# Sums of both halves of the queries and both heads of a pair on four column tiles, an earlier second load, and two moves around the mixer

## Chip, cores, metric

One NeuronCore of a Trainium2 chip. The metric is device microseconds (us) of one execution. Each figure is a median of several executions; most executions of one kernel agree within 0.3%. "Half clock" below means stretches in which the trace records a granted clock of TensorE of 0.5.

## The reference, cut to what matters

```python
# hash attention: B=4, H=8 heads, S=768, D=64, 6 hash bits
mask   = bucket(q @ proj)[..., :, None] == bucket(k @ proj)[..., None, :]
scores = where(mask, q @ k.T / 8, -1e9)
attn   = exp(scores - max);  attn = attn / (sum(attn) + 1e-9)
x      = (attn @ v) as (B, S, 512)
# mixer
u   = x + (relu(x.T @ w_tok1) @ w_tok2).T      # token mixing
out = u + relu(u @ w_ch1) @ w_ch2              # channel mixing
```

## The kernel before, in the parts that matter

Attention goes over 16 pairs of heads (two heads side by side on the 128 partitions), and in each pair over two halves of 384 queries. For a half, TensorE makes scores in six chunks of keys, ScalarE takes the exponentials `e`, GpSimd and VectorE add the six chunks (`esa`, `esd`), TensorE sums over keys with a matrix of ones (`sums`), ScalarE and VectorE turn this into a factor by logarithm, exponential and one Newton step, TensorE weighs the values (`acc`), ScalarE moves `acc` to `num`, and GpSimd multiplies `num` by the factor into `XT`. Sums and weighing of a half are issued during the next half.

```python
            def sums(self):
                ps = psum.tile([P, 512], F32, name="sums", tag="sm", bufs=1)[:, :HALF]
                for i in range(2):                                   # the two heads
                    nc.tensor.matmul(ps[D*i : D*i+D], ones, self.d[:, i], start=True, stop=True)
                # near = exp(-ln(ps)) on ScalarE
            def newton(self):
                # rec = (ps * near - 2) * near: two VectorE operations of 128x384
...
        for n in range(len(pairs)):
            for half in range(2):
                now = Half(n, half); now.scores()
                now.add(0)                      # GpSimd: e0+e1; VectorE: e2+e3+e4
                if before: before.sums()
                if half == 0 and n + 1 < len(pairs):
                    hashes(n + 1)               # ends in 8 small transfers of bits on the SP queue
                    load_qk(n + 2)
                ...
                if before: before.newton()
                now.add(1)                      # VectorE: +e5, then +esa
                if n:
                    weights.some(third)         # a third of one weight block's conversion
                    third = (third + 1) % 3
                if before: before.weigh()       # TensorE acc, ScalarE num, GpSimd division
```

The weights arrive as 64-bit floats and are converted in blocks of 768 KB, one third of the work in each half:

```python
        def begin(self):   # third 0: ScalarE reads raw (the block that has landed), VectorE two operations
        def join(self):    # third 1: VectorE, then GpSimd two operations of 128x768
        def end(self):     # third 2: ScalarE a square, VectorE the last operation (L196), which frees raw
        def some(self, k):
            (self.begin, self.join, self.end)[k]()
            if k == 2:
                self.fetch()                    # request of the next block into the only raw buffer
```

So the request of a block waits for VectorE's L196, and one half later ScalarE, an in-order queue, must have the block before it may move `acc` or take exponentials.

## Time and profile before

886.32 us, median of three runs; the profiled one has a span of 883.2 us. By stage:

| stretch, us from the start | length | TensorE busy | granted clock |
|---|---|---|---|
| 0 to 27.93 (to the first sums) | 27.93 | 18.1 | 0.88 |
| to 347.32 (attention) | 319.39 | 317.6 | 1.00 |
| to 442.47 (token mixing) | 95.15 | 91.7 | 1.00 |
| to 883.20 (channel mixing) | 440.73 | 433.6 | 1.00 |

The start is the one stretch with large gaps. The prediction shows the lines behind this.

### The profile page before, as it was taken

The numbers are of one execution on the slowest core, as the hardware profiler recorded it, in microseconds if no ns is written. First come the engines' busy times: TensorE is split into PE (matmuls) and PEld (weight loads), VectorE is DVE, ScalarE is ACT, GpSimd is POOL, SyncE is SP. The second block draws the span as 40 slices with busy tenths as digits, with TensorE's granted clock in tenths as the row PEclk, the third lists the DMA queues.
The fourth block names the chain that finished last, engine by engine and source line by source line (L and its number), as shares of the span: only waits on it lengthen the run. The fifth ranks groups of instructions, "written<-read, shape, count | busy, mean of one in ns | idle before, by whom it ended". The sixth has DMA issues, their size and how long they took to land.

```text
span 883.2 us, 9198 instructions
## 1 busy us (share of the span) xinstructions
PE 861.0 (97%) x3505; PEld 394.2 (45%) x3505; DVE 494.6 (56%) x576; ACT 321.4 (36%) x477; POOL 243.8 (28%) x156
## 2 busy tenths in 40 slices
PE   5999999999999999999999999999999999999997
PEld 2444444444444445455534444444444444444443
DVE  2666776776677554589975464435448342336411
ACT  2676776667777665424311210001210101211000
POOL 3253544354444222547611111101111200111110
PEclk9999999999999999999999999999999999999999
DMA  5223323322322203223301211131120120000001
GB/s 177 79 75 110 112 87 151 126 99 85 111 110 75 74 3 108 71 72 108 107 1 36 72 36 60 52 127 38 70 71 1 59 84 24 0 1 0 24 24 51
DMA packets 20500, 61.14 MB, mean 69 GB/s; under 512 B 2785, under 2 KB 4193, under 8 KB 20449
## 3 DMA queue, kind: packets, MB, share of 16 engines
q1 hardware_dynamic: 20392, 60.46, 19.8%
q8 instruction: 29, 0.48, 0.2%
q14 instruction: 23, 0.18, 0.1%
q10 hardware_dynamic: 56, 0.02, 0.0%
HBM read 53.49 MB, written 6.29 MB: 68 GB/s over the span
## 4 chain that ended last, share of the span: by engine, by line
PE 90%; DVE 4%; DMA 2%; ACT 1%; issue 1%; SPq 1%; POOL 0%; DVEq 0%; ACTq 0%
PE b L587 48%; PE sc L299 16%; PE acc L363 13%; PE t L522 4%; PE sums L343 3%; PE t L535 2%; PE hp L266 2%; DMA qk<-in_qk 1%; PE trp L226 1%; SPq L280 1%; DMA raw<-in_moe_w_tok 1%; DVE XT L541 1%; DVE WC L196 1%; DVE tmp L170 1%; ACT e L306 1%
## 5 line engine op out<-in xcount | busy, mean ns | idle before, releaser
L299 PE MATMUL sc<-qk 64*128 64x384 f32 x768 | 161.9, 501 | 2.5 <-ACT e L306 2.5
L306 ACT ACTIVATE e<-sc 128x768 f32<-128x768 f32 x192 | 150.4, 813 | 28.7 <-PE sc L299 28.7
L594 ACT COPY p<-b 128x512 f32<-128x512 f32 x72 | 42.2, 586 | 295.5 <-PE b L587 295.5
L363 PE MATMUL acc<-e,vn 128*64 128x384 f32 x768 | 130.0, 488 | 0.0
L587 PE MATMUL b<-r,WC 128*128 128x512 f32 x288 | 125.6, 592 | 0.0
L587 PE MATMUL b<-T,SW 128*128 128x512 f32 x216 | 97.0, 593 | 1.7 <-DVE T L677 0.9
L299 PEld LDWEIGHTS sc<-qk 64*128 64x128 f32 x768 | 67.8, 190 | 61.1 <-issue 45.9
L331 DVE TENSOR_TENSOR esd<-e 128x768 f32<-128x768 f32 x32 | 41.2, 1289 | 93.5 <-ACT e L306 93.5
L613 POOL TENSOR_TENSOR p<-p,p 128x512 f32<-128x512 f32 x18 | 25.5, 1415 | 238.9 <-ACT p L594 238.9
L363 PEld LDWEIGHTS acc<-e,vn 128*64 128x64 f32 x768 | 53.9, 137 | 72.4 <-issue 72.2
L587 PEld LDWEIGHTS b<-r,WC 128*128 128x128 f32 x288 | 54.7, 190 | 68.9 <-issue 66.5
L329 POOL TENSOR_TENSOR esa<-e 128x768 f32<-128x768 f32 x32 | 66.4, 2076 | 33.7 <-ACT e L306 33.7
L371 POOL TENSOR_TENSOR XT<-num,rec 128x384 f32<-128x384 f32 x32 | 39.1, 1221 | 125.8 <-ACT num L368 87.5
L587 PE MATMUL b<-T,WC 128*128 128x512 f32 x144 | 67.7, 593 | 0.1
L587 PEld LDWEIGHTS b<-T,SW 128*128 128x128 f32 x216 | 40.9, 190 | 54.0 <-issue 50.7
L185 POOL TENSOR_TENSOR tmp<-tmp,raw 128x768 f32<-128x768 f32 x20 | 41.0, 2052 | 86.0 <-DVE tmp L182 48.8
L587 PE MATMUL b<-XT,WC 128*128 128x512 f32 x144 | 64.7, 592 | 0.0
L299 PE MATMUL sc<-bits 64*128 64x384 bf16 x384 | 63.5, 324 | 0.0
L587 PE MATMUL b<-r,SW 128*128 128x512 f32 x144 | 62.8, 592 | 0.0
L617 DVE TENSOR_TENSOR r<-p,u 128x512 f32<-128x512 f32 x18 | 12.5, 692 | 87.2 <-ACT u L594 86.7
L368 ACT ACTIVATE num<-acc,vsum 128x384 f32<-128x384 f32 x32 | 18.6, 580 | 71.2 <-PE acc L363 71.2
L535 PE MATMUL t<-W,r 128*128 128x384 f32 x128 | 42.3, 488 | 1.6 <-DVE XT L541 1.6
(81 smaller groups left out, 955.5 us busy)
## 6 DMA issues: line engine op xcount, KB each, us to landing
raw<-in_moe_w_ch SPq DMA_DIRECT2D x16, 768.0 KB
seen<-in_qk SPq DMA_DIRECT2D x16, 768.0 KB
qk<-in_qk SPq DMA_DIRECT2D x15, 768.0 KB
vn<-in_v SPq DMA_DIRECT2D x16, 384.0 KB
vt<-in_vT SPq DMA_DIRECT2D x16, 384.0 KB
out<-p SPq DMA_DIRECT2D x18, 256.0 KB
raw<-in_moe_w_tok SPq DMA_DIRECT2D x4, 768.0 KB
bits<-g SPq DMA_DIRECT2D x124, 5.2 KB
```

What stands on the lines that cost most here:

```text
L185: nc.gpsimd.tensor_tensor(unit, unit, lo, op=ALU.mult)
L299: nc.tensor.matmul(sc[:, i, :HALF], t[rows, 1, P * c : P * c + P], t[rows, 0, qs], start=start, stop=not start,)
L306: nc.scalar.activation(e, sc[:, :, :HALF], ACT.Exp, scale=SCALE)
L329: nc.gpsimd.tensor_tensor(self.a, es[0], es[1], op=ALU.add)
L331: nc.vector.tensor_tensor(self.d, es[2], es[3], op=ALU.add)
L343: nc.tensor.matmul(ps[D * i : D * i + D], ones, self.d[:, i], start=True, stop=True,)
L363: nc.tensor.matmul(acc[D * i : D * i + D], vn[:, i, c], e[:, i], start=(c == 0), stop=(c == NR - 1),)
L371: nc.gpsimd.tensor_tensor(XT[:, hp, at : at + HALF], num, self.rec, op=ALU.mult)
L522: nc.tensor.matmul(ps, W1[:, r, P * j : P * j + P], x[:, r], start=(r == 0), stop=(r == NR - 1),)
L535: nc.tensor.matmul(ps[:, :HALF], r1[:, j, P * cb : P * cb + P], W2[:, j, HALF * half : HALF * half + HALF], start=(j == 0), stop=(j == NJ ...
L587: nc.tensor.matmul(self.ps[i], left(k), right(k), start=first and k == ks[0], stop=k == ks[-1], skip_group_check=True,)
L594: nc.scalar.copy(c, self.ps[i])
```

## The change

Its intent: fill four column tiles of TensorE with sums instead of two, so that one pass does both halves of a pair; take the second pair's load out of TensorE's way; keep TensorE's clock open with idle matmuls at the start; make two of the four block differences of channel mixing during token mixing; and shorten the tail. Cut to its core:

```diff
-            def sums(self):            # once per half: 2 matmuls of 64 columns
+        class Quotients:               # once per pair, in the first half of the next pair
+            def sums(self):
+                for i in range(2):
+                    for h in range(2):
+                        at = 32 * (2 * i + h)
+                        nc.tensor.matmul(ps[at:at+32], ones[:, :32], self.halves[h].d[:, i], ...)
+            def newton(self):
+                nc.vector.tensor_tensor(t, ps, near, op=ALU.mult)
+                for h in range(2):
+                    nc.vector.scalar_tensor_tensor(rec[:, h], t, 2.0, near, ...)
+                for i in range(2):
+                    for h in range(2):
+                        at, other = D*i + 32*h, D*i + 32*(1-h)
+                        nc.vector.tensor_copy(rec[other:other+32, h], rec[at:at+32, h])
+            def divide(self):          # one GpSimd operation of 128x768 instead of two of 128x384
+                nc.gpsimd.tensor_tensor(XT[...], nums.pop(self.n), self.rec, op=ALU.mult)
...
+        load_qk(1)                     # ahead of the first bits' transfers, was behind load_v(0)
+        idle = psum.tile(...)
+        for _ in range(14):
+            nc.tensor.matmul(idle[:D, :D], ones, ones, start=True, stop=True)
...                                     # token mixing, after its third batch:
+            if b == 2:
+                inputs(0, T, 0)        # two of four differences; T is now four tiles, was one
...                                     # last output block:
+                for cols in parts:     # two halves of 256 columns
+                    x.product(3, ..., cols)
```

More of the change, by code (lines that the diff above doesn't have):

```diff
@@ L78 @@
     assert S == 6 * P and DM == 512 and NB <= 8 and DTOK % P == 0 and DCH % P == 0
-    assert B * NP % 2 == 0 and B * S % (2 * TT) == 0
+    assert 2 * TT <= 2 * S and B > 2 and B * NP % 2 == 0 and B * S % (2 * TT) == 0
     SCALE = 0.125
@@ L329, in add @@
                     nc.gpsimd.tensor_tensor(self.a, es[0], es[1], op=ALU.add)
-                    self.d = pool.tile([P, 2, HALF], F32, name="esd", tag="esd", bufs=2)
+                    self.d = pool.tile([P, 2, HALF], F32, name="esd", tag="esd", bufs=3)
                     nc.vector.tensor_tensor(self.d, es[2], es[3], op=ALU.add)
@@ L337, in add @@
                     )
-            def sums(self):
-                ps = psum.tile([P, 512], F32, name="sums", tag="sm", bufs=1)[:, :HALF]
-                for i in range(2):
-                    nc.tensor.matmul(
-                        ps[D * i : D * i + D], ones, self.d[:, i], start=True, stop=True,
-                    )
-                near = pool.tile([P, HALF], F32, name="near", tag="near", bufs=2)
-                nc.scalar.activation(near, ps, ACT.Ln)
-                nc.scalar.activation(near, near, ACT.Exp, scale=-1.0)
-                self.ps, self.near = ps, near
-            def newton(self):
-                ps, near = self.ps, self.near
-                rec = self.rec = pool.tile([P, HALF], F32, name="rec", tag="rec", bufs=2)
-                nc.vector.tensor_tensor(rec, ps, near, op=ALU.mult)
-                nc.vector.scalar_tensor_tensor(rec, rec, 2.0, near, op0=ALU.subtract, op1=ALU.mult)
             def weigh(self):
@@ L366, in weigh, with __init__ @@
                         )
-                num = pool.tile([P, HALF], F32, name="num", tag="num", bufs=2)
-                nc.scalar.activation(num, acc, ACT.Identity, scale=-1.0, bias=vsum)
+                if self.half == 0:
+                    nums[self.n] = pool.tile([P, 2, HALF], F32, name="num", tag="num", bufs=2)
+                nc.scalar.activation(
+                    nums[self.n][:, self.half], acc, ACT.Identity, scale=-1.0, bias=vsum,
+                )
+        nums = {}
+        class Quotients:
+            def __init__(self, halves):
+                self.n, self.halves = halves[0].n, halves
+            def sums(self):
+                ps = psum.tile([P, 512], F32, name="sums", tag="sm", bufs=1)[:, :HALF]
+                for i in range(2):
+                    for h in range(2):
+                        at = 32 * (2 * i + h)
+                        nc.tensor.matmul(
+                            ps[at : at + 32], ones[:, :32], self.halves[h].d[:, i], start=True, stop=True,
+                        )
+                near = pool.tile([P, HALF], F32, name="near", tag="near", bufs=1)
+                nc.scalar.activation(near, ps, ACT.Ln)
+                nc.scalar.activation(near, near, ACT.Exp, scale=-1.0)
+                self.ps, self.near = ps, near
+            def newton(self):
+                ps, near = self.ps, self.near
+                t = pool.tile([P, HALF], F32, name="t", tag="t", bufs=1)
+                rec = self.rec = pool.tile([P, 2, HALF], F32, name="rec", tag="rec", bufs=2)
+                nc.vector.tensor_tensor(t, ps, near, op=ALU.mult)
+                for h in range(2):
+                    nc.vector.scalar_tensor_tensor(
+                        rec[:, h], t, 2.0, near, op0=ALU.subtract, op1=ALU.mult,
+                    )
+                for i in range(2):
+                    for h in range(2):
+                        at, other = D * i + 32 * h, D * i + 32 * (1 - h)
+                        nc.vector.tensor_copy(rec[other : other + 32, h], rec[at : at + 32, h])
+            def divide(self):
@@ L369, in weigh @@
                 b, hp = pairs[self.n]
-                at = S * b + HALF * self.half
-                nc.gpsimd.tensor_tensor(XT[:, hp, at : at + HALF], num, self.rec, op=ALU.mult)
+                nc.gpsimd.tensor_tensor(
+                    XT[:, hp, S * b : S * b + S].rearrange("p (h q) -> p h q", h=2),
+                    nums.pop(self.n), self.rec, op=ALU.mult,
+                )
         nc.scalar.preload_act_table_set("natural_log_exp_and_others")
@@ L377, in attention @@
             nc.gpsimd.memset(t, 0.0)
+        load_qk(1)
+        idle = psum.tile([P, 512], F32, name="idle", tag="sm", bufs=1)
+        for _ in range(14):
+            nc.tensor.matmul(idle[:D, :D], ones, ones, start=True, stop=True)
         hashes(0)
         load_v(0)
-        load_qk(1)
         load_v(1)
@@ L386, in attention @@
         )
-        before = None
+        before, both = None, []
         third = 0
@@ L395, in attention @@
                 now.add(0)
-                if before:
-                    before.sums()
+                quotients = None
+                if len(both) == 2:
+                    quotients, both = Quotients(both), []
+                    quotients.sums()
+                both.append(now)
                 if half == 0 and n + 1 < len(pairs):
@@ L402, in attention @@
                     add_values(n + 1)
-                if before:
-                    before.newton()
+                if quotients:
+                    quotients.newton()
                 now.add(1)
@@ L410, in attention @@
                     before.weigh()
+                if quotients:
+                    quotients.divide()
                 if half == 0:
@@ L417, in attention @@
         turn(0, x0, lambda: psum.tile([P, 2, 512], F32, name="trp", tag="sc", bufs=3))
-        before.sums()
-        before.newton()
+        quotients = Quotients(both)
+        quotients.sums()
+        quotients.newton()
         before.weigh()
+        quotients.divide()
     def careful_attention(pool, psum):
@@ L495, in careful_attention, with inputs, tokens @@
                 flip(XT[:, hp, at : at + P], [x])
-    def tokens(pool, psum, W1, W2, x0, weights, jobs):
+    def inputs(s, T, which):
+        a, b = (slice(TT * (2 * s + i), TT * (2 * s + i) + TT) for i in range(2))
+        low, high = slice(0, NCB // 2), slice(NCB // 2, NCB)
+        if which == 0:
+            nc.vector.tensor_tensor(T[0], XT[:, low, b], XT[:, low, a], op=ALU.subtract)
+            nc.vector.tensor_tensor(T[2], XT[:, high, b], XT[:, low, b], op=ALU.subtract)
+        else:
+            nc.vector.tensor_tensor(T[1], XT[:, high, b], T[0], op=ALU.subtract)
+            nc.vector.tensor_tensor(T[3], XT[:, high, a], T[1], op=ALU.subtract)
+    def tokens(pool, psum, W1, W2, x0, weights, jobs, T):
         x1 = pool.tile([P, NR, DM], F32, name="x1", tag="x1", bufs=1)
@@ L570, in weight_sums, with channels @@
         return [early, late]
-    def channels(pool, psum, SW1, WC2, SW2, judge):
+    def channels(pool, psum, SW1, WC2, SW2, T, judge):
         KC, HC = NCB // 2, NHT // 2
-        T = pool.tile([P, 4 * KC, TT], F32, name="T", tag="T", bufs=1)
+        T = [T[0], None, T[1], None]
+        for i in (1, 3):
+            T[i] = pool.tile([P, KC, TT], F32, name=f"T{i}", tag=f"T{i}", bufs=1)
         class Blocks:
@@ L582, in __init__, with product @@
                 self.copies = {}
-            def product(self, i, left, right, ks, first):
+            def product(self, i, left, right, ks, first, cols=slice(0, TT)):
                 ks = list(ks)
@@ L587, in product @@
                     nc.tensor.matmul(
-                        self.ps[i], left(k), right(k),
+                        self.ps[i][:, cols], left(k), right(k)[:, cols],
                         start=first and k == ks[0], stop=k == ks[-1], skip_group_check=True,
@@ L605, in hidden @@
             x.product(1, lambda k: WC1[:, KC + k, low], lambda k: XT[:, KC + k, sl[0]], ks, True)
-            x.product(2, lambda k: WC1[:, k, high], lambda k: T[:, k], ks, True)
-            x.product(3, lambda k: SW1[:, 1, k, low], lambda k: T[:, 2 * KC + k], ks, True)
+            x.product(2, lambda k: WC1[:, k, high], lambda k: T[0][:, k], ks, True)
+            x.product(3, lambda k: SW1[:, 1, k, low], lambda k: T[2][:, k], ks, True)
             p1 = x.copy(0, "p1")
@@ L610, in hidden @@
             p5 = x.copy(2, "p5")
-            x.product(0, lambda k: SW1[:, 0, k, low], lambda k: T[:, KC + k], ks, False)
+            x.product(0, lambda k: SW1[:, 0, k, low], lambda k: T[1][:, k], ks, False)
             p7 = x.copy(3, "p7")
@@ L614, in hidden @@
             x.product(2, lambda k: SW1[:, 2, k, low], lambda k: XT[:, KC + k, sl[1]], ks, False)
-            x.product(3, lambda k: WC1[:, KC + k, high], lambda k: T[:, 3 * KC + k], ks, False)
+            x.product(3, lambda k: WC1[:, KC + k, high], lambda k: T[3][:, k], ks, False)
             u = x.copy(0, "u")
@@ L633, in outputs @@
             for r, t in zip(rs, ks):
-                nc.vector.tensor_tensor(T[:, t], r[:, 3], r[:, 1], op=ALU.subtract)
+                nc.vector.tensor_tensor(T[t // KC][:, t % KC], r[:, 3], r[:, 1], op=ALU.subtract)
                 nc.vector.tensor_tensor(r[:, 1], r[:, 1], r[:, 0], op=ALU.subtract)
@@ L643, in outputs @@
                 x.product(2, lambda k: WC2[:, k, high], lambda k: rs[k][:, 1], ks, True)
-                x.product(3, lambda k: SW2[:, 1, k, low], lambda k: T[:, k], ks, True)
+                x.product(3, lambda k: SW2[:, 1, k, low], lambda k: T[k // KC][:, k % KC], ks, True)
                 p1 = x.copies["p1"]
@@ L651, in outputs @@
             if s + 1 < B * S // (2 * TT):
-                inputs(s + 1)
+                inputs(s + 1, T, 0)
+                inputs(s + 1, T, 1)
             for _ in range(3):
@@ L657, in outputs @@
                 x.product(2, lambda k: SW2[:, 2, k, low], lambda k: rs[k][:, 3], ks, False)
-                x.product(3, lambda k: WC2[:, HC + k, high], lambda k: rs[k][:, 2], ks, False)
+                final = s == last and m == KC - 1
+                parts = [slice(0, TT // 2), slice(TT // 2, TT)] if final else [slice(0, TT)]
+                for cols in parts:
+                    x.product(3, lambda k: WC2[:, HC + k, high], lambda k: rs[k][:, 2], ks, False, cols)
                 u = x.copy(0, "u")
@@ L666, in outputs @@
                 nc.sync.dma_start(out=out[m, :, sl[1]], in_=p5)
-                nc.vector.tensor_tensor(u, x.ps[3], u, op=ALU.add)
-                nc.sync.dma_start(out=out[KC + m, :, sl[0]], in_=u)
-        def inputs(s):
-            a, b = (slice(TT * (2 * s + i), TT * (2 * s + i) + TT) for i in range(2))
-            low, high = slice(0, KC), slice(KC, NCB)
-            t1, t2, t3, t4 = (T[:, KC * i : KC * i + KC] for i in range(4))
-            nc.vector.tensor_tensor(t1, XT[:, low, b], XT[:, low, a], op=ALU.subtract)
-            nc.vector.tensor_tensor(t3, XT[:, high, b], XT[:, low, b], op=ALU.subtract)
-            nc.vector.tensor_tensor(t2, XT[:, high, b], t1, op=ALU.subtract)
-            nc.vector.tensor_tensor(t4, XT[:, high, a], t2, op=ALU.subtract)
+                for cols in parts:
+                    nc.vector.tensor_tensor(u[:, cols], x.ps[3][:, cols], u[:, cols], op=ALU.add)
+                    at = slice(sl[0].start + cols.start, sl[0].start + cols.stop)
+                    nc.sync.dma_start(out=out[KC + m, :, at], in_=u[:, cols])
         unseen = list(range(len(pairs))) if judge else []
@@ L706, in decide @@
             return rest
-        inputs(0)
+        inputs(0, T, 1)
         last = B * S // (2 * TT) - 1
@@ L746, in attention_and_tokens @@
         SW2 = big["SW2"] = pool.tile([P, 3, NHT // 2, DM // 2], F32, name="SW2")
+        T = big["T"] = [pool.tile([P, NCB // 2, TT], F32, name=f"T{i}") for i in (0, 2)]
         def weights(pool):
@@ L766, in jobs @@
             ]
-        inside(tokens, W1, W2, x0, weights, jobs)
+        inside(tokens, W1, W2, x0, weights, jobs, [T[0], None, T[1], None])
     def careful_attention_and_tokens(W1, W2, x0):
@@ L781, in careful_attention_and_tokens @@
         inside(turned)
-        inside(tokens, W1, W2, x0, None, None)
+        inside(tokens, W1, W2, x0, None, None, [big["T"][0], None, big["T"][1], None])
     with_token_weights(attention_and_tokens)
-    inside(channels, big["SW1"], big["WC2"], big["SW2"], True)
+    inside(channels, big["SW1"], big["WC2"], big["SW2"], big["T"], True)
     flag = nc.values_load(unsafe, min_val=0, max_val=1)
@@ L788 @@
         with_token_weights(careful_attention_and_tokens)
-        inside(channels, big["SW1"], big["WC2"], big["SW2"], False)
+        inside(channels, big["SW1"], big["WC2"], big["SW2"], big["T"], False)
 _WEIGHTS = ["moe_w_tok1", "moe_w_tok2", "moe_w_ch1", "moe_w_ch2"]
```

## The prediction

> **What bounds the kernel now.** I read the page's engine shares first, then the stretches by stage, then the chain that ended last, then TensorE's waits, and last the single records where two of these disagree. Shares (columns: busy us, share of the span, instructions):
> ```profile
> PE 861.0 (97%) x3505; PEld 394.2 (45%) x3505; DVE 494.6 (56%) x576; ACT 321.4 (36%) x477; POOL 243.8 (28%) x156
> PE 90%; DVE 4%; DMA 2%; ACT 1%; issue 1%; SPq 1%; POOL 0%; DVEq 0%; ACTq 0%
> ```
> TensorE is the bound, and the chain of waits agrees: 90% of the end is TensorE's own work. So a change pays only where it takes TensorE time away or closes one of its gaps. The stretches by stage (start-up, rest of attention, token mixing, channel mixing) show where gaps exist:
> ```profile
> 0.00:28.00 28.00, 18.18 (x90) 7.61 (x92) 7.52 (x12) 10.51 (x14) 9.09 (x18) 0.88 0.43 144
> 28.00:348.00 320.00, 318.21 (x2114) 145.78 (x2115) 213.67 (x251) 221.03 (x327) 129.35 (x77) 1.00 0.26 91
> ```
> Columns: span, busy us of PE, PEld, DVE, ACT, POOL, granted clock, DMA share, GB/s. The first 28 us lose 9.8 us of TensorE and run partly at half clock (0.88 on average); attention afterwards has almost no gap, so there only removed TensorE work counts. TensorE's waits name the gaps:
> ```profile
> PE hp L266 <- DMA qk<-in_qk: 9.1, 2, 4.9
> PE sc L299 <- ACT e L306: 2.5, 5, 0.9
> PE b L587 <- DVE T L677: 0.9, 1, 0.9
> PE b L587 <- DVE T L676: 0.8, 1, 0.8
> ```
> The 9.1 us are the first two hashes. 4.9 us is the first pair's load, which nothing moves; the other 4.2 us is the second pair's load. In the chain in order of time (start, us, what):
> ```profile
> 12.93 6.74 DMA qk<-in_qk
> 19.81 1.51 PE hp L266 x8
> 21.32 6.68 PE sc L299 x36
> ...
> 37.71 0.80 PE sums L343 x4
> 38.51 0.78 PE hp L266 x8
> 39.29 4.02 PE acc L363 x24
> 43.31 5.05 PE sc L299 x36
> 48.35 0.80 PE sums L343 x4
> 49.15 3.87 PE acc L363 x24
> ```
> Here one pair of heads is seen: a first half of scores, sums, hashes, weighing, and a second half without hashes. Sums are 0.80 us, 32 times. Scores of 36 records take 5.05 us, but 6.68 us at 21.32, where the clock was granted at half from 17.76 to 24.59 us after TensorE had idled from about 15.5 to 19.8.
>
> **What the Trainium skill says.** "TensorEngine Tiling (Array Packing)", section Tiling Modes, says that a column dimension of 32 allows four tiles and that changing the tiling mode drains TensorE. The trace agrees on both: in the single records four hash matmuls start 6 to 7 ns apart and one pass of all four takes 0.32 us, as does a pass of two tiles of 64 in the sums; and from scores to sums 0.256 us pass where the step inside scores is 0.16, so a switch costs about 0.1 us. "TensorE: Matmul & The Clock Gate", Part 1, says the array starts at half clock and needs about 3.4 us of sustained activity, and that idle windows bring half clock back; the trace agrees (half clock until 10.9 us, then again as above). "GPSIMD Engine Reference", section Key points, says GpSimd shares its SBUF interfaces with VectorE for VectorE operations with two SBUF inputs or in a two-port mode; the trace agrees: the 128x768 final conversion multiply takes 0.95 us alone and 1.75 us at 64.86, ending 0.8 us after GpSimd's division.
>
> **The change, part by part.**
>
> *Sums.* Single records of a first half before: sums' first pass 0.37, second pass with the switch 0.42, hashes 0.35 and 0.44, together 1.58 us. After, the order of instructions puts four 32-column sums straight before the four 32-column hashes, the same mode: 0.35 + 0.32 + 0.32 + 0.44 = 1.43. That saves 0.15 us, 14 times: 2.1 us. In a second half the sums (0.70 us from first to first record) vanish, but weighing then pays the switch, 0.05: 0.65 saved, 16 times: 10.4 us. The two sums without hashes behind them cost 0.05 more each. Sum: 12.4 us off TensorE. Note that the chain's 32 x 0.80 = 25.6 us halved would be 12.8, nearly the same.
>
> Of this, some comes back. Four times in attention TensorE waits because ScalarE's in-order queue stands at a weight block that has not landed:
> ```profile
> 74.75 0.94 ACT L165 ACTIVATE raw<-raw 128x768 f32<-128x768 uint32 x1 [3.33 <-DMA raw<-in_moe_w_tok]
> 75.57 0.57 ACT L368 ACTIVATE num<-acc,vsum 128x384 f32<-128x384 f32 x1
> 76.04 2.22 ACT L306 ACTIVATE e<-sc 128x768 f32<-128x768 f32 x3
> ```
> ScalarE stood 3.33 us, then num and the exponentials came late; the next scores took 6.22 us instead of 5.05 (the others 5.69, 5.52, 5.63). These gaps sum to 1.17 + 0.64 + 0.47 + 0.58 = 2.9 us. Each follows a first half in which the block was requested at its end, behind eight small bit transfers of 0.735 us each on the issuing queue. After, that landing is fixed by the hash, the queue and VectorE, while TensorE arrives 0.15 + 0.65 = 0.8 us sooner. So each gap grows by about 0.8. On top, VectorE's Newton step per pair of halves is now one 0.55 product, two 0.56 and four copies of 32x384, which I estimate at 0.3 to 0.4 each from the 0.55 us of a 128x768 single-input operation here: about 3.0 us instead of 1.1, all in the first half, ahead of the operation that releases the block. Before, that operation ended at 66.6 and the request left at 68.48, so 1.9 us of slack; the extra 1.9, plus a 128x768 division on GpSimd (about 2.1 from the esa row's 2076 ns) contending with it, eats this and perhaps 0.3 more. I book 0.9 x 4 = 3.6 us given back. Net of the sums: 8.8 us.
>
> *Second pair's load earlier.* The first loads stream near 400 GB/s and finish at 5.8 us, and the queue is then empty until 9.5. The second 768 KB, issued near 2.6, should land near 8, long before the hash needs it (15.6). The bit transfers start after 8.4, so nothing is delayed. The 4.2 us gap closes; without it there should be no half clock there: hashes 1.44 to 0.78 (0.66) and scores 6.68 to 5.05 (1.63). Sum 6.5 us. The value loads behind keep their place (they landed by 15.9; ScalarE wants the second at 16.4).
>
> *Fourteen idle matmuls.* Roughly 28 passes of about 0.11 us at half clock, from 1.0 to 4.1 us, before the first load lands: free. They may open the clock early, which saves up to 0.9 us in the hashes ahead of the first bits. But scores then finish sooner and TensorE idles two microseconds for the bits, which can bring half clock at a worse place (2.5 to 3 us). I book -0.4 on balance: 6.1 us for the start.
>
> *Block sums earlier.* Before, channel mixing's first products waited 0.27 + 0.92 + 1.08 = 2.3 us for T. After, two of four subtractions (1.22 us each) run in token mixing and the other two come before they are needed. But VectorE is itself close to the bound there: from 407 to 424 it goes through conversions, mostly waiting for GpSimd, and 2.4 us more may reach the additions into XT, for which TensorE already waits at 430.9 and 437.2 (about 1 us each). If the delay passes through whole, the gain is nil; if it fits in the waits, 2 us. I book 0.6.
>
> *Last output in halves.* The last addition shrinks from 0.69 to about 0.42 (estimate: half the elements plus the fixed part) and the last transfer from 256 to 128 KB, about 0.35 us at 400 GB/s. Twelve more matmuls of half width cost about nothing. 0.6 us.
>
> Total 8.8 + 6.1 + 0.6 + 0.6 = 16.1 us; with chances that lean to more than less at the start (its clean value is 6.5 to 7.4), I put the time at 869.5 us, 1.9% less.
>
> **Rivals.** (1) *The sums' gain is kept whole*: the weight block lands earlier because GpSimd no longer divides at the end of second halves, so the hash's bits (held 1.0 us by GpSimd at 60.6) leave earlier. For it: that hold recurs at 122.9, 184.6 and 246.1, just before the four gaps. Against it: VectorE's longer Newton step. Gaps would stay near 1.3 us; time about 866. (2) *VectorE becomes the bound in first halves*: its work there is about 10 us of 10.5 with contention, and copies start in different partitions, so may be held. Gaps of 2 us at four places, or new ones in every pair: 873 to 878. Against: second halves leave it some 3 us idle, and what it makes late is used five or more us later. (3) *Half clock moves rather than goes*: start gains 4 instead of 6; 872. (4) *Token mixing returns nothing, or loses a microsecond*: 870 to 871.
>
> **Range and chances.** The start is uncertain by 1.5 us, the given-back gaps by 2, token mixing by 1, together about 2.7: 865.3 to 873.5 holds eight in ten. The 2% line is 868.6, just under my number: faster by over 2% 0.40, within 2% 0.59, slower 0.01.
>
> **What would show it.** Sums 16 times, some 1.43 us for sums and hashes together; second halves 9.07 us from scores to scores; the second hash without a DMA wait and followed by scores of about 5.1 us; clock near 1 from 11 us on; scores after a block's landing longer than 5.05 by 1.3 to 2 us at four places; no wait of the first products for T, but longer waits in token mixing for XT. I am wrong if the scores of ordinary pairs show new waits for ScalarE or VectorE, or if those four gaps don't grow.

## The result

888.91 us (887.57 to 890.64, four runs) against 886.54 of the kernel before on the same chip. The ratio is 1.0028, 95% interval 1.0006 to 1.0051: the same by the 2% rule, slightly slower in fact, and 19 us above my number. Ratios here are the mean time of one kernel's runs over that of the other's of the same rounds, so not quite the ratio of the medians quoted.

First the stage views of both kernels, cut at the same events. First start and attention of the changed kernel, then attention of the kernel before (span, busy us of PE, PEld, DVE, ACT, POOL, clock, DMA share, GB/s):
```profile
0.00:24.08 24.08, 19.86 (x116) 9.92 (x117) 7.14 (x12) 10.65 (x14) 9.11 (x18) 0.86 0.51 167
24.08:353.02 328.94, 314.03 (x2115) 145.01 (x2113) 258.69 (x295) 204.73 (x294) 135.88 (x61) 0.98 0.26 89
```
```profile
27.93:347.32 319.39, 317.60 (x2114) 145.41 (x2112) 213.10 (x250) 220.60 (x326) 129.35 (x77) 1.00 0.26 92
```
The start is 3.85 us shorter. Attention is 9.55 us longer although TensorE does less in it, its clock is 0.98, and VectorE is busy 45.6 us more. Token mixing grew by 1.98 and channel mixing shrank by 2.18. Sum: +5.5 us, the difference of the two profiled spans.

TensorE's waits in the changed kernel (us in total, times, longest):
```profile
PE sc L299 <- ACT e L306: 15.5, 5, 3.8
PE t L583 <- DVE XT L589: 3.3, 3, 1.6
PE hp L266 <- DMA qk<-in_qk: 0.9, 2, 0.6
```
The wait for the second pair's load is gone, as planned. But the wait of scores for ScalarE went from 2.5 to 15.5 us. In the chain of work that ended last the shares by engine are now:
```profile
PE 81%; DVE 10%; DMA 3%; ACT 2%; issue 2%; POOL 1%; SPq 0%; DVEq 0%; ACTq 0%
```
TensorE fell from 90 to 81%, VectorE rose from 4 to 10%. The first of the four places, in the changed kernel, on ScalarE and then on TensorE (start, us, what, in brackets the idle time before and what ended it):
```profile
71.54 0.93 ACT L165 ACTIVATE raw<-raw 128x768 f32<-128x768 uint32 x1 [6.59 <-DMA raw<-in_moe_w_tok]
72.37 0.56 ACT L351 ACTIVATE num<-acc,vsum 128x384 f32<-128x384 f32 x1
72.83 2.19 ACT L306 ACTIVATE e<-sc 128x768 f32<-128x768 f32 x3
```
```profile
69.59 0.33 PE L299 MATMUL sc<-bits 64*128 64x384 bf16 x2
73.67 1.65 PE L299 MATMUL sc<-qk 64*128 64x384 f32 x4 [3.75 <-ACT e L306]
...
75.43 1.49 PE L299 MATMUL sc<-qk 64*128 64x384 f32 x4
...
76.95 0.81 PE L299 MATMUL sc<-qk 64*128 64x384 f32 x4
```
ScalarE stood 6.59 us at the weight block (3.33 before). TensorE filled its three score buffers and waited 3.75 us. Then it ran at half clock: four records took 1.65 and 1.49 us instead of 0.81. The clock record shows half from 73.44 for 3.41 us. The same happens at 138.3, 203.1 and 268.0. The four scores took 10.62, 10.37, 10.66 and 10.68 us, where they took 6.22, 5.69, 5.52 and 5.63 before: 19.3 us.

Why did the block come late? VectorE in the half that releases it, before and then after:
```profile
57.33 1.12 DVE L331 TENSOR_TENSOR esd<-e 128x768 f32<-128x768 f32 x1 [3.50 <-ACT e L306]
58.56 1.57 DVE L332 TENSOR_TENSOR esd<-esd,e 128x768 f32<-128x768 f32 x1
...
63.98 0.96 DVE L335 SCALAR_TENSOR_TENSOR esd<-esd,esa 128x768 f32<-128x768 f32 x1
64.86 1.75 DVE L196 SCALAR_TENSOR_TENSOR W<-raw,tmp 128x768 f32<-128x768 f32 x1
```
```profile
52.04 2.30 DVE L331 TENSOR_TENSOR esd<-e 128x768 f32<-128x768 f32 x1 [2.33 <-ACT e L306]
54.45 2.40 DVE L332 TENSOR_TENSOR esd<-esd,e 128x768 f32<-128x768 f32 x1
...
59.23 1.45 DVE L390 COPY rec<-rec 32x384 f32<-32x384 f32 x4
...
61.77 2.38 DVE L335 SCALAR_TENSOR_TENSOR esd<-esd,esa 128x768 f32<-128x768 f32 x1
64.08 2.58 DVE L196 SCALAR_TENSOR_TENSOR W<-raw,tmp 128x768 f32<-128x768 f32 x1
```
and GpSimd beside it, after:
```profile
51.71 1.82 POOL L186 TENSOR_TENSOR tmp<-tmp 128x768 f32<-128x768 f32 x1
53.49 2.55 POOL L329 TENSOR_TENSOR esa<-e 128x768 f32<-128x768 f32 x1
60.82 2.51 POOL L394 TENSOR_TENSOR XT<-num,rec 128x768 f32<-128x768 f32 x1 [4.79 <-DVE rec L390]
63.30 2.54 POOL L329 TENSOR_TENSOR esa<-e 128x768 f32<-128x768 f32 x1
```
GpSimd's four operations end at 53.53, 56.04, 63.34 and 65.84; the four long VectorE operations end at 54.34, 56.85, 64.15 and 66.65, each 0.81 us later. None of the four overlaps GpSimd in any useful sense: each waits until GpSimd's operation has ended and then does its own work. GpSimd is held in its turn: its division took 1.81 us in `no_copies` (below), where no VectorE operation ran as it began, and 2.51 us here, where VectorE's first addition (L334) was still running. That is what the Trainium skill says in "SBUF — State Buffer", section SBUF: two separate sides: the port pair that the two engines share is an exclusive lock for the whole instruction, and VectorE operations with two SBUF inputs contend for it with a GpSimd operation that reads SBUF. I had read only the milder sentence that the prediction cites.

Measured from the start of that half's scores, mean of the four places:

| event | before | after |
|---|---|---|
| Newton step begins on VectorE | 8.91 | 10.03 |
| L196 ends, the block's buffer is free | 13.65 | 19.09 |
| request of the next block leaves | 15.52 | 19.15 |
| ScalarE begins the new block | 21.36 | 23.82 |
| the next first half's scores are due | 20.36 | 19.56 |

The release is 5.44 us later: 1.12 before the Newton step (the two additions that waited for GpSimd, less a hold of the hash operation of about 1 us that is gone at the first of the four places), 2.07 in the Newton step with its copies, 1.43 in the two additions behind it (all of it in the second, L335) and 0.82 in L196 (both beside GpSimd). 1.81 of it fell into slack, since before the request stood behind the bit transfers, and the landing was 1.17 quicker; the block is 2.46 us later and TensorE wants it 0.80 sooner. That is 3.26 us more wait, and with 1.6 us of half clock behind it 4.8 us at each of four places.

### The profile page after: what moved, and what is told of

It is laid out like the page before. It is cut to its first block, busy times and chain, and to the rows that moved or that the text cites. A ratio compares the mean times of both kernels' runs of the same rounds, so it can differ in the third digit from the quotient of the medians.

```text
span 888.7 us, 9246 instructions
## 1 busy us (share of the span) xinstructions
PE 858.7 (97%) x3545; PEld 398.6 (45%) x3545; DVE 543.7 (61%) x625; ACT 305.6 (34%) x445; POOL 249.6 (28%) x140
## 4 chain that ended last, share of the span: by engine, by line
PE 81%; DVE 10%; DMA 3%; ACT 2%; issue 2%; POOL 1%; SPq 0%; DVEq 0%; ACTq 0%
PE b L639 49%; PE sc L299 13%; PE acc L345 10%; PE t L570 4%; PE t L583 3%; DMA raw<-in_moe_w_tok 2%; DVE esd L335 2%; ACT e L306 1%; PE sums L369 1%; DVE WC L196 1%; DMA raw<-in_moe_w_ch 1%; DVE tmp L170 1%; PE hp L266 1%; PE trp L226 1%; DVE rec L390 1%
## 5 line engine op out<-in xcount | busy, mean ns | idle before, releaser
L299 PE MATMUL sc<-qk 64*128 64x384 f32 x768 | 166.9, 514 | 15.9 <-ACT e L306 15.5
L639 PE MATMUL b<-r,WC 128*128 128x512 f32 (+1 forms) x300 | 125.6, 575 | 0.0
L665 POOL TENSOR_TENSOR p<-p,p 128x512 f32<-128x512 f32 x18 | 22.9, 1271 | 238.9 <-ACT p L646 238.9
L329 POOL TENSOR_TENSOR esa<-e 128x768 f32<-128x768 f32 x32 | 71.0, 2224 | 67.3 <-ACT e L306 67.3
L639 PEld LDWEIGHTS b<-r,WC 128*128 128x128 f32 x300 | 57.0, 190 | 67.1 <-issue 64.1
L331 DVE TENSOR_TENSOR esd<-e 128x768 f32<-128x768 f32 x32 | 37.1, 1159 | 49.1 <-ACT e L306 49.1
L669 DVE TENSOR_TENSOR r<-p,u 128x512 f32<-128x512 f32 x18 | 12.4, 691 | 86.7 <-ACT u L646 86.7
L394 POOL TENSOR_TENSOR XT<-num,rec 128x768 f32<-128x768 f32 x16 | 37.5, 2346 | 77.1 <-ACT num L351 39.7
L335 DVE SCALAR_TENSOR_TENSOR esd<-esd,esa 128x768 f32<-128x768 f32 x32 | 52.8, 1649 | 9.7 <-POOL esa L329 6.8
L186 POOL TENSOR_TENSOR tmp<-tmp 128x768 f32<-128x768 f32 x20 | 46.0, 2302 | 1.6
```

Source lines behind the costliest of these rows:

```text
L186: nc.gpsimd.tensor_tensor(big, big, unit, op=ALU.add)
L299: nc.tensor.matmul(sc[:, i, :HALF], t[rows, 1, P * c : P * c + P], t[rows, 0, qs], start=start, stop=not start,)
L329: nc.gpsimd.tensor_tensor(self.a, es[0], es[1], op=ALU.add)
L331: nc.vector.tensor_tensor(self.d, es[2], es[3], op=ALU.add)
L335: nc.vector.scalar_tensor_tensor(self.d, self.d, NR * EPS, self.a, op0=ALU.add, op1=ALU.add,)
L394: nc.gpsimd.tensor_tensor(XT[:, hp, S * b : S * b + S].rearrange("p (h q) -> p h q", h=2), nums.pop(self.n), self.rec, op=ALU.mult,)
```

## The experiments

Sixteen kernels. Theory A: the late release of a weight block, and half clock behind the wait, make the whole loss. Rivals: the loss is at the start or in token mixing (B), or VectorE and GpSimd are simply too full (C and E).

### The sums alone, and everything but the sums

`sums_only` is the kernel before with the classes above changed; `rest_only` is the changed kernel with the old sums. One thing of the mixer stays in `sums_only`: T is four tiles, and its trace still has the two earlier differences in token mixing (see the small terms below).

```diff
 # sums_only
-        load_qk(1); idle matmuls            # start as before
-                inputs(0, T, 0)             # in token mixing
-                final = s == last and m == KC - 1
+                final = False
```

> The kernel before with the sums part of the change alone (start, block sums and last output as before). Theory A (the change makes the release of a weight block late at four places, ScalarE stands at it, TensorE waits about 3.7 us and then runs at half clock): the whole loss is here, attention about 9.5 us longer than before, time 894 to 898 us, four scores of 10 to 11 us. Rival B (the four-tile sums are sound and the loss comes from the start or from the block sums moved into token mixing): time below 884 us, no scores over 6.5 us.

> The change without its sums part: earlier load of the second pair, idle matmuls, block sums in token mixing, last output in halves. Theory A: the start's 3.9 us gained, the other parts about nil, time 881.5 to 884 us. Rival B: no gain or a loss, 886 us or more.

Measured: 894.92 us, ratio 1.0095 (1.0067 to 1.0124), with four scores of 10.36, 10.64, 10.25 and 11.99 us; and 882.88 us, ratio 0.9959 (0.9936 to 0.9982). Both as theory A has it: the loss is in the sums part, and the rest gains. Rival B is out: `rest_only` has the new start and the new token mixing and loses nothing. The granted clock of `rest_only` was 0.998, and one of its four places took 9.88 us in the profiled run, with an unchanged release (13.6 us) but a block that ScalarE began 2.4 to 2.9 us later than at the others: one late landing, whose cause I don't know, is enough to open such a wait with the old sums too. It may be why `rest_only` gains less than the earlier load alone (`load_early` below, 0.9925); the three runs without a trace can't say.

### A second buffer for weight blocks

```diff
-            bufs=1,
+            bufs=2,
-            if k == 2:
+            if k == 0:
                 self.fetch()
```
(One `tmp` buffer here, and in the changed kernel one `rec` buffer, so that it fits.)

> The changed kernel with two buffers for incoming weight blocks in attention, so that a block is requested two halves before ScalarE wants it and no longer waits for VectorE's release (one conversion buffer and one for the quotients' factors as before or less, to fit). Theory A: all four waits go, each 5.6 us, time 864 to 869 us, clock 0.99 or more throughout attention. Rival C (VectorE and GpSimd are simply too full in first halves, and the waits go elsewhere): scores of some pairs stay over 6 us, time 875 us or more.

> Control: the kernel before with the same second buffer. Theory A: its four small waits (2.9 us in sum) go, 883 to 884.5 us. If it gained 8 us or more, the buffer would do something else than theory A says.

Measured: 872.98 us, ratio 0.9858 (0.9839 to 0.9878), clock 1.000; and 882.50 us, ratio 0.9962 (0.9943 to 0.9981). The four waits are gone in both, and between these two the change is worth 1.0% instead of costing 0.3 (0.9858 over 0.9962); the kernel before gained 0.5 us more than I had written down. But 872.98 is 4 us over the upper end of what theory A expected. The profile shows a new wait of TensorE, and behind it one of VectorE:
```profile
PE sums L369 <- DVE esd L335: 6.3, 4, 1.7
```
```profile
DVE esd L335 <- POOL esa L329: 13.9, 4, 3.5
```
In the halves where GpSimd has a conversion and then the division in front of the addition `esa`, VectorE's last addition waits for that, and the four-tile sums wait for VectorE. So rival C is partly right: with the first wait gone, a second one stands behind it.

### GpSimd's division moved behind the next half's addition

```diff
                 now.add(0)
+                if half and quotients:
+                    quotients.divide()
                 quotients = None
...
-                if quotients:
-                    quotients.divide()
```

> The changed kernel with a second weight buffer, and the division of a pair moved behind the next half's first GpSimd addition instead of ahead of it. In after_two_raw four sums waited about 1.6 us each for a VectorE addition that waited 3.5 us for GpSimd, which had a conversion and the division in front of the addition it needed. Theory A2 (GpSimd's order makes this wait): the four waits go, 6.3 us, 865 to 868 us. Rival (VectorE's own work is what is late there): waits stay, 872 us or more.

> The changed kernel with the division alone moved, one weight buffer as in the change. Theory A with GpSimd contention as one of its causes: VectorE's last addition (2.4 us beside the division) takes 1 us again and the release 1 to 1.8 us, so the weight block is requested about 2.2 us sooner, the four waits shrink from 3.7 to about 1.5 us and half clock does not follow: about 3.5 us each, 873 to 877 us. If contention has no part: 887 us or more.

Measured with two buffers: 869.06 us, ratio 0.9813 (0.9796 to 0.9829); at the four places sums and hashes together take 1.99 us instead of 3.74 to 3.92 (1.43 is what they take without a wait), so the order on GpSimd made most of that wait. But three other pairs now take 2.42 and one 1.87: over 1.43, all pairs together lose 5.7 us instead of 10.0, so more than half of the wait moved or stayed. The time is a little over what I expected. With one buffer: 888.28 us, ratio 1.0042 (1.0017 to 1.0067), where I expected 873 to 877. A miss, and the trace shows why. The next half's exponentials are there sooner than I thought, so the moved division still runs beside VectorE's last addition (2.40 us again), and the `esa` that now comes first holds one copy for 1.9 to 2.0 us instead of 0.35. The release came 19.7 us after the scores' start at three places (19.0 at the fourth), later than the 19.1 of the change. Moving work about on GpSimd doesn't help as long as VectorE's release stands behind all of it.

### Without the copies

```diff
-                for i in range(2):
-                    for h in range(2):
-                        at, other = D * i + 32 * h, D * i + 32 * (1 - h)
-                        nc.vector.tensor_copy(rec[other : other + 32, h], rec[at : at + 32, h])
```

> The changed kernel without the four copies of 32x384 per pair (wrong result on purpose: half of the factors are those of the other half of the queries). Theory A: the block is requested 1.45 us sooner, the four waits go from 3.7 to 2.2 us; [...]half clock should not follow: 3.0 us each, 875 to 878 us; if half clock still follows, 882 to 884 us. Rival D (copies lie beside other work and cost nothing): 888 us.

Measured: 879.89 us median, four runs of 878.86 to 880.71 and one of 888.38; ratio 0.9933 (0.9917 to 0.9950). So the copies cost 8 to 9 us of time, though they are 1.45 us on an engine that is busy 61%. The value lies between the two that I wrote down. The release came 2.7 us sooner (16.4), not 1.45. The two operations behind the copies were still held:
```profile
58.75 2.57 DVE L335 SCALAR_TENSOR_TENSOR esd<-esd,esa 128x768 f32<-128x768 f32 x1
61.24 2.57 DVE L196 SCALAR_TENSOR_TENSOR W<-raw,tmp 128x768 f32<-128x768 f32 x1
```
The rest of the gain lies ahead of the Newton step, which began at 8.7 instead of 10.0 us, in part because the hash operation (L274) was no longer held at three of the four places (0.32 us instead of 1.3). The profiled run is the slow one of the five; in it the block needed 6.4 to 7.5 us from its request, just behind the next pair's load, so its waits were as long as in the change. What a landing costs varies, and I can't read the four good runs' waits from a trace.

### TensorE kept busy in the four waits

```diff
                     exponential(sc)
+                    if c == 2 and self.half == 0 and self.n in (3, 6, 9, 12):
+                        warm = psum.tile([P, 512], F32, name="warm", tag="sm", bufs=1)
+                        for _ in range(32):       # 14 in keep_warm_short
+                            nc.tensor.matmul(warm[:, :P], ident, ident, start=True, stop=True)
```

> The changed kernel with 32 small matmuls (about 3.4 us) put on TensorE into each of the four waits, so that it waits but does not idle. Theory A with half clock as a part of the loss: the waits stay at 3.7 us, the scores behind them run at full clock, 1.6 us less each, 881 to 884 us, granted clock 0.995 or more. If half clock does not come from the idle wait: no change or a loss, 888 us or more.

> The changed kernel with 14 small matmuls in each of the four waits; keep_warm had 32, which took 7.3 us instead of the 3.4 I had reckoned (two passes of 0.107 us each), longer than the wait. 14 take 3.0 us, within the wait of 3.7. Theory A with half clock as a part: waits as before, the second 18 records of the scores behind take 2.6 instead of 4.25 us, 4 x 1.6 = 6.4 us less than the changed kernel, 881 to 884 us. If half clock were no part: 888 us or more.

Measured: with 32 matmuls 896.64 us, ratio 1.0118 (1.0101 to 1.0135): my filler was twice too long, 7.4 us, so it lengthened the waits and tells nothing of the time. With 14: 882.34 us, ratio 0.9954 (0.9935 to 0.9973), clock 0.998. On TensorE at the first place:
```profile
67.51 3.39 PE L326 MATMUL warm<-ident 128*128 128x128 f32 x28
71.17 0.92 PE L299 MATMUL sc<-qk 64*128 64x384 f32 x4 [0.27 <-ACT e L306]
...
72.89 0.81 PE L299 MATMUL sc<-qk 64*128 64x384 f32 x4
```
The scores come as late as in the change, but behind the wait they take 0.81 us again. Against the change (1.0028) that is 0.74%, 6.6 us, against 6.4 expected. Not all of it is from the four places: there the scores took 8.90, 9.14, 8.95 and 9.44 us, 5.9 us less in sum than in the change, and the profiled run of the change also had half clock at the start, which this one hasn't. The trace has no half clock at the four places any more, so it came from the idle wait, and it is three tenths of the loss there.

### The conversion's third moved ahead

This takes away the late release itself: no buffer added, copies and division as in the change.

```diff
                 now.add(0)
+                if n:
+                    weights.some(third)
+                    third = (third + 1) % 3
...
                 now.add(1)
-                if n:
-                    weights.some(third)
-                    third = (third + 1) % 3
```

> The changed kernel with each half's third of a weight conversion moved ahead of the sums, the hashes and the quotients: VectorE releases the block before its longer Newton step and the request stands ahead of the bit transfers on the issuing queue. Theory A (the release behind the Newton step, copies and division is the cause): release near 10 us after the start of the half's scores instead of 19, landing near 15 instead of 23.8, all four waits gone with half clock behind them, 864 to 869 us, with one buffer and unchanged copies and division. Rival E (VectorE and GpSimd are too full, so moving one operation only moves the wait): other waits of 1 us or more appear in many pairs, 875 us or more.

> Control: the same move in the kernel before. Its four waits of 2.9 us in sum should go, 882.5 to 884.5 us, as with the second buffer.

Measured: 867.16 us, ratio 0.9775 (0.9759 to 0.9791), faster than both kernels; and 882.49 us for the kernel before with the same move, ratio 0.9952 (0.9935 to 0.9968), so that the change is worth 1.8% on top of it. The same half in `weights_first`, on VectorE and on the transfers' queue:
```profile
53.29 0.94 DVE L196 SCALAR_TENSOR_TENSOR W<-raw,tmp 128x768 f32<-128x768 f32 x1
```
```profile
54.26 0.38 SPq L154 DMA_DIRECT2D raw<-in_moe_w_tok  x1
```
L196 ends 9.0 to 9.4 us after the scores' start instead of 19.1, and ScalarE begins the next block at 16.4 without a wait that reaches TensorE: scores for ScalarE wait 0.7 us in all, no score but the first takes over 5.2 us, and the clock is 0.999. Theory A is shown: the release is what made the four waits. VectorE is busy even longer here, 560 us, so fullness alone (rival E) was not the cause.

### The load alone

> The kernel before with the second pair's load ahead of the first bit transfers, and nothing else. As I booked it: the 4.2 us wait and the half clock behind it go, 879.5 to 881 us, so more than half of what the whole start was booked at. If the load is hidden anyway: 885 us or more.

```diff
             nc.gpsimd.memset(t, 0.0)
+        load_qk(1)
         hashes(0)
         load_v(0)
-        load_qk(1)
```

Measured: 880.13 us, ratio 0.9925 (0.9908 to 0.9941), clock 0.998 to 1.000. One line moved gives 6.4 us by the medians, as booked for the load with its clock.

### The small terms, on `weights_first`

> weights_first without the fourteen idle matmuls, taken against weights_first in the same rounds (867.2 us in its own). If the idle matmuls are free or useful as booked: 867 to 868 us. If they bring half clock to a worse place in part of the runs: weights_first spreads more, and this is 0.5 to 2 us faster in the mean, with a narrower spread.

> weights_first with the last output whole, as before. As I booked it, 0.6 us slower, 867.8 us. In the profile of the change both half additions start only after the last matmul, so my guess now is no difference: 866.5 to 867.5 us.

> weights_first with all four block sums at the start of channel mixing, as before. In the profile of the change token mixing grew by 2.0 us and channel mixing's first part shrank by 2.5: 0.5 us slower, 867.7 us; within noise of weights_first if the two cancel.

> weights_first with the division behind the next half's first GpSimd addition. If the sums of every third pair wait because that addition stands behind a conversion and the division: the five waits of 0.5 us go, about 2.5 us less, 864 to 866 us. If VectorE's own work makes them: 867 us, no change.

Each leaves out or changes one part in the lines shown above. Medians of five runs: 867.28, 866.61, 867.03 and 866.97 us; ratios 0.9782, 0.9780, 0.9786 and 0.9791, all with intervals of about 0.0013 to either side, so none is told apart from the others. `weights_first` itself was not in these rounds; its 0.9775 was taken in others. The idle matmuls and the halved last output are worth nothing that these runs can show.

The earlier block differences were not tested. `wf_no_t_early` puts their call back into channel mixing, but in its trace the two still run in token mixing, 42.6 and 35.7 us before the first channel product (in the kernel before, all four run after it):
```profile
384.32 1.32 DVE L540 TENSOR_TENSOR T<-XT 128x1024 f32<-128x1024 f32 x1
391.28 2.84 DVE L541 TENSOR_TENSOR T<-XT 128x1024 f32<-128x1024 f32 x1
```
So the place of the call in the source doesn't decide when they run once T is four tiles, and no run has the four tiles without early differences. Always check in the trace that an edit did what it was meant to do.

`wf_late_divide` was expected to give 2.5 us and gave nothing, because the waits of the sums moved: in `weights_first` sums and hashes take 0.45 to 0.63 us over 1.43 in seven pairs, in `wf_late_divide` 0.46 in one pair and about 1.0 in three, 3.7 and 3.6 us in sum.

## Why the prediction was wrong

*The sums' own saving* was right. Attention's +9.55 us, less 19.3 at the four places, less 2.0 (four times 0.5, where sums and hashes took 1.94 instead of 1.43 us because the second half's sums waited for VectorE), less 0.4 of one score, leaves -12.1; I had 12.4.

*The step that failed* is the one that booked "0.9 x 4 = 3.6 us given back". I had the mechanism and the four places, and mis-sized it: 4.8 x 4 = 19.3, and 2.4 us of smaller waits. Even its own terms, 0.8 and 0.3, add up to 1.1 and not 0.9. Inside it three terms:

1. The release. I wrote that VectorE's longer Newton step plus contention "eats this and perhaps 0.3 more", some 2.2 us of delay. It was 5.4. The Newton step with its copies was right (3.12 us against "about 3.0"). What I missed is the lock: I counted contention as part overlap, where the last addition and L196 waited out GpSimd's whole operations (2.25 us). The division took 2.5 us and not the 2.1 that I took from a mean, which mixed operations that were held with others that were not. And the additions ahead of the Newton step lost time too (1.1), where my rival 1 had expected a gain.
2. The landing. It was quicker than before, 4.7 against 5.8 us from the request, and this gave back 1.2 us that I hadn't booked. The next pair's load left 3.0 us ahead of the request instead of 0.5; that this is the reason isn't shown, since in `no_copies` it left 1.6 us ahead and the block took longer, 6.4 to 7.5 us.
3. Half clock. I had read in the same trace that a wait at the start brought it, but reckoned it only there. The four waits of about 1 us before had not brought it; those of 3.7 us did, and by the scores of `keep_warm_short` it is 5.9 us in all.

Rival 2 of the prediction named the right place ("gaps of 2 us at four places") and was still far too small: it said 873 to 878.

*The start* was booked at 6.1 and gave 3.9 in the profiled run: half clock from 12.0 to 18.8 us, as rival 3 says, at the scores behind the first bits. The prediction had named this danger beside the idle matmuls and booked 0.4 for it; it cost 2.5 (these scores took 10.83 us, in `after_two_raw` 8.33). It comes in some runs and not in others: of twelve profiled kernels with the idle matmuls three show it, of the two with the earlier load and no idle matmuls none. Without that it was 6.4 to 6.9 (`load_early` by its time, `after_two_raw` by its first weighing at 21.03). Of the changed kernel's four runs two had a clock of 0.987 (889.99 and 890.64 us) and two of 0.990 and 0.991 (887.83 and 887.57), which fits half clock at the start in two of them; only the first was profiled.

*Block differences* (0.6 booked): token mixing grew by 1.98 us, where TensorE's waits for XT went from 1.6 to 3.3 us, and channel mixing shrank by 2.18, where the waits for T (0.9 and 0.8) are gone. So most of the delay passed through, as the prediction feared, and what is left is small; no run isolates it. *The last output* (0.6) was wrong: nothing. In the changed kernel's trace the first half's addition starts after the last matmul of the second:
```profile
883.09 0.76 DVE L724 TENSOR_TENSOR u<-b,u 128x256 f32<-128x256 f32 x2 [4.49 <-PE b L639]
```
Both halves stand together; the end is 6.01 us after the last matmul's start, 5.93 before. Why the first addition waits, whether for the whole bank or something else, I haven't tested.

What stays open: how much each of copies and lock is worth alone (without the copies the lock's share changes too), the waits of the sums of about 0.5 us in seven pairs of `weights_first`, and what the earlier block differences are worth.

## What to carry to other kernels

Work taken off the engine that sets the end pays only if the others can hand over sooner; here the same change made TensorE want a block 0.8 us earlier and VectorE free its buffer 5.4 us later. So follow each buffer that the moved work stands in front of: the operation that frees it, the request behind that, and who stands still in order at its landing. In an in-order queue put the operation that releases a transfer ahead of long work that nobody waits for: this one move turned +0.3% into -2.2%.

## What the Trainium skill lacked or had wrong

- "GPSIMD Engine Reference", section Key points, speaks of contention with no size. "SBUF — State Buffer", section SBUF: two separate sides, has the rule (an exclusive lock, the other fully blocks), and the runs agree: 128x768 operations with two inputs took 2.3 to 2.6 us instead of 0.95, each ending 0.81 us after GpSimd's. The first page gives no size, and neither gives one for operations like these. Here two GpSimd operations of 2.5 us back to back held two VectorE operations in a row, 4.9 us for 1.9 us of work; of GpSimd's 2.5 us some 0.7 were its own wait for VectorE (1.81 alone).
- "TensorE: Matmul & The Clock Gate", Part 1, has half clock after at least one idle window of about 3.4 us. The page doesn't say how busy is busy. In each trace here the clock records begin on a grid of 3.41 us. Cutting all eighteen traces on their grids shows it: of the stretches at full clock in which TensorE was busy for 0.42 or less, all 20 were followed by half clock (the start of the kernel before, 0.38, among them); of 33 between 0.45 and 0.6, three (0.54 to 0.55, at the start); of 4450 busier ones, none. So the length of a wait alone doesn't decide: the change's waits of 3.5 to 3.8 us brought half clock, each for 3.41 us, but a wait of 3.59 us in `late_divide` fell across two stretches (busy 0.49 and 0.45) and brought none.
- "TensorEngine Tiling (Array Packing)", section Tiling Modes, says that a change of mode drains TensorE and gives no time. Here it was about 0.1 us (0.256 us from scores to sums, 0.16 from scores to scores), and putting two groups of the same mode side by side saved 0.15 us a pair.
